# A sparse-attention and mixing kernel: a new issue order for all engines, two accumulator banks for the angles, sine products allowed on GpSimd

## The chip, the cores and the metric

The kernel runs on one core of a Trainium2 chip. The core has a matrix engine (TensorE, "PE" in the profile, with its weight loads "PEld"), three elementwise engines (VectorE "DVE", ScalarE "ACT", GpSimd "POOL") and a synchronisation engine (SyncE "SP") that issues all of this kernel's DMA transfers. Each engine takes its instructions in program order from a queue of its own and waits on semaphores for the results of the others. TensorE writes into PSUM, a small memory of eight banks; all else works in SBUF.

The metric is the device time of one execution in microseconds (us). A run is one execution that is timed.

## What is computed

Two stages follow one another. The first is attention with 4 batches, 8 heads, 768 positions and 64 channels a head. Each position sees its 31 nearest positions and 24 summaries of blocks of 32 positions (the maximum of the keys, the mean of the values). The second stage turns the 512 channels of each position by angles, mixes all positions, and ends with a channel product.

```python
scores_l = scale * np.matmul(q, k.transpose(0, 1, 3, 2))          # masked to |i - j| < 16
scores_s = scale * np.einsum('bhsd,bhnd->bhsn', q, k_sum) + np.log(block)
a = softmax(np.concatenate([scores_l_m, scores_s], axis=-1))
x = np.matmul(a, np.concatenate([v, v_sum], axis=2))              # then [B, S, 512]
theta = x @ w_theta
zr, zi = x * np.cos(theta), x * np.sin(theta)
y = np.einsum('ts,bsd->btd', w_tok_r, zr) + np.einsum('ts,bsd->btd', w_tok_i, zi)
u = x + y
out = u + np.maximum(u @ w_ch, 0.0)
```

## The kernel before

**Tiles.** Each batch has six tiles of 128 positions, 24 tiles in all, numbered b * 6 + i. A tile passes through these steps, each of them one or several operations:

- scores (line 1658): TensorE multiplies queries with 118 keys a query group: 94 neighbours and 24 summaries. VectorE adds the mask and takes the row's extreme (line 1684), ScalarE takes the exponentials (line 1688).
- the probabilities' transposition. For tiles 0 to 5 TensorE transposes them into the PSUM bank "p" (line 1693) and a copy brings them to SBUF (line 1516). From tile 6 on `turn_words` (line 1665) does it without TensorE: a copy splits each 32-bit word into 16-bit halves ("part", line 1516), one transposing DMA turns all of them (line 1674), and a second copy joins the halves ("join", line 1516, tiles `pt` and `zx`). There are 54 such transfers: two a tile for the probabilities, one a tile for x.
- the value product (line 1700), a small addition, a reciprocal and a multiplication that normalises (lines 1704 to 1713). The result is the tile's x.
- x is transposed in the same two ways (line 1725 or `turn_words`), split into a high part and a low part (lines 1516 and 1522), and stored to a scratch tensor in DRAM.
- angles (`theta_tile`, line 1751): twelve matmuls into the PSUM bank "t" (line 1757), a reduction to a full turn (lines 1765 to 1768), cosine and sine on ScalarE (lines 1779 and 1780), the products with x (line 1787, "sine products", two a tile, 48 in all), and their high and low parts (`split_z`).

High and low parts exist because TensorE's fast 32-bit product keeps fewer bits than the result needs. So a product of two 32-bit factors is made as three matmuls: high by high, high by low, low by high.

**Mixing.** `mix_step` (line 1803) adds one tile's share to three PSUM accumulators `m0` to `m2`. One batch needs two halves of six steps. Batch 0 uses line 1800, the other batches line 1835. At the end of a half, VectorE adds x back (line 1848) and the sum goes to DRAM. `out_unit` (line 1862) loads it again, splits it and makes the channel product (line 1878) with the last addition (line 1883); there are eight such units.

**Weights.** The weights come as 64-bit floats. `load_f64` (line 1551) decodes each of 32 pieces by hand: a magnitude (lines 1563 and 1565), two clamping and shifting steps (lines 1567 and 1568), two combining steps (lines 1570 and 1572), and the high and low parts.

**Order.** `Program.op` records each operation with its readers and writers and with the letters of the engines it may run on; it does not issue it. There are 2,460 operations. `Program.issue` (line 1477) then issues them in the order of the long string `ORDER` (from line 52 on). A row of it is an engine's letter (P, A, V, G, S for PE, ACT, DVE, POOL, SP) and a list of steps: "+2" means the operation two numbers after the last one. So the string fixes two things: the engine of each operation that may run on several, and the place of every operation in its engine's queue. 40 warm-up matmuls (line 1547) on a blank tile are part of the list.

The constant `DT = 6` in line 1491 is the tile from which the transposing transfers are used. `bank(tag, shape)` names a PSUM bank; a new user of a bank waits until the readers of the one before it are done.

```python
            for word in seqs:
                n = n + int(word[1:]) if word[0] == "+" else n - int(word[1:]) if word[0] == "-" else int(word)
                o = self.ops[n]
                o.fn(e)
```

Of the kernel before, what the change touches and what calls it, by code (L numbers as in the profile page):

```python
# [20 lines left out]
P = 128  # L21
# [32 lines left out]
V+1,+1,+1,+1,+1  # L54
A+1
G+1
V-107
S+43,+65
A+1
S-64  # L60
G-43
V+44,-2
S+3,-51
P+7,+1,+1,+1
S+43,+15
P-57,+1,+1,+1,+1
V+37,-47,+49
S+74,-127
V+113,+1
S-60,+2  # L70
P+18
V-4,+45
A+13
V-51
S-19,+4
V+29
S-31,-59
A+80
V-5,+40,-27,-16,+5
A+4,+13  # L80
S-31
G+65
V+1
S+21
A-34
V+14
A-38
V-18,+57,-42
A+43,-53
P-65  # L90
A+64
V+13,+26
A-22
V+38
S+213
P-292,+2,+2,+2,+2,+2
A+1,+6,+22
P-78,+67
V+69
S-81,-3,+51,+232,+398  # L100
V-596,+1
P+200
V-270,+71,+201,-200
A+196
G-283
P+16
V+1,+1,+268,+3
A+2,-203
P-60,-80,+1
G+140,+192  # L110
P-331,+1,+1
A+67
V+10,+259,+12
A-10,+3
V-242,+630,-380
A-9
P-262
A+274
P-351,+1
A+77  # L120
V+1,+252,+19
P-9,-339
S+111
A+1
S+31,+236
V-32
A+4,-1
P-349,+1,+1
S+212,+166
V-403,+100  # L130
A+274,-12
P-37,+79
G-285
S+227,-77
V-149,+1,+14
G+212
V-225
A+204,+1,-204
G+1
V+12,+192,+79  # L140
P-44,+12
V+44,+3,-58
S-183
P+149,+1
V+77
A-242
P+166,+1
V+72,+1
A+4,+2
V+9,-56  # L150
A+46,-2
V-242
A+209
P+37
V-47
A+59
P-399,+351
A-43
V-197,+31
A+255  # L160
V-3
A+4
V-255
G+166
A+91
S-285,+312,-240
P+243
V-318,+198
S+66
V-263,+275  # L170
A-77,+41
P-351
V+352,+1
P+35
A-77
V+121
P-78
V-211
S+107
A+105,+34  # L180
P-388,+1
G+111
P+287
V-256
A+212
V+75
S+283
G-357
V-212,+285
S-284,+281  # L190
V-115,+121
A-246
S+241,-266
V+228
A+47,-123
V+401,-271,+1
A-290,+293
P-89
V-171,+125
G-157  # L200
V+33,+257,-256
A+246,-2
V+13,-56,-234
A+244,+34
V-244
P+169,+1,+1
A+1
P+39
V-244
A+291  # L210
P-11
V-74,-205
A+292,-1,-47
V-87,+88
A+35
V-247
G+1
V+172
S+113
P+3  # L220
S-215
A-106
V+323
P-31
A-47
P-402,+403,+34
V+42,+2
S-4,+50
A-164
V+132  # L230
A-383
V+381,+1,-336,-45
A+291,-260,+220,+135,-49,+35,+12
P-496,+1,+1
A+495
V-2,-382,+368,-44,-323
G+627
V-337,+1
P+124
V-91  # L240
A+45,+2
V-370,+29,+221
P+42,+1,+1,+1
V-46,+75,-126
A+98
P+39,-447,+1
A+478
P+4
A+13,-48
S+249,+20,-530  # L250
V-45,+166,-195,+30,-29
A+42
G+1
V+252,+40
S+23
A-22
V+77,-383
A+1
V+265,+120
A-46,-73  # L260
P+40
A+1,+82,-81
P-451
V+156,+370,-382,+42
S+507,-572,+280
P+82,-482
G+186
P-185
V+155
G+295  # L270
P+2
V+242,-169
A-117,+315,-194,-168
V-205,+30,+1,+295,-294,+222,-1
A-252
P+336,-492,+1,+1,+450,+1
A+40
V-11
A+45,+193
V-182  # L280
P-84
V+29
P+11
S-204
V+401
P-119
V-77,+42,-1
A-81,-97
V+138
A-308  # L290
V+1
A+530
G-562,+204,+360
S-475,+454
G+23
A-197,+14,+1
G-85
P+115,-568,+1
V+453
A-338  # L300
P+411
G-410
A+377,+34,-73
P+40,+76
V+127
A-202
V-378,+418
S-20,-353,+532,-178
A+22,+1
V-421,+1  # L310
S+653
V-652,+1
P+599,-154
V+155
A-225
G+1
A-42
S-253
V+493,+28
S-31  # L320
P-164
A+1
G+216
A-20
P-185
V+182
P-223,+1,+1,+68
V-406,+577,+68,-84
S-278
V+11  # L330
S+252
V-16
G+88,-617
V+1
G+617
V-326
A+272
V-562,+1,+188
A+186,+186
P-225  # L340
A+224
V-196
S+170,-358
V+397,-208,-363,+569,+1
A-235,-95
G+96,+275
P-208,+3
G+206
P-238,+241
G-614  # L350
V+374,+1,-39,+40,+156
P-124
A-171,+324
P-184
V+1,+1,-88,+343,-3
S-98
A+40,-1
S-51
A+53,+1,+2
S-34  # L360
V-9,-500,+488,+20,-250
A-3
S+289
A-241,+1
G-98
P+171
V+198,+8,-582,+1,-10,+11,+302
P+64
G-165
P+168,-2,+3  # L370
G+138,-165
A+258
P-224,+123
A+1,+6
G-254,+381
P-261
V+208
A-277,+281
P-240,+1
V-345,+503,+67,-268  # L380
S+99,+123
A+1,-524
P+378
S+187,+62
A-31,-14
S-604
P+367,+1
S-296
V+253,-315,+316,-303
A+346  # L390
V-358,+1
P+535
V+1,-535
S-45
A+594,-593
V+580,+1
S-186,-340,+8
A+621
P-257,+3
A-385  # L400
V+585,-1
P-195,-1
V+214
A-14,+18
V-250,+245,-244
G-401,+682,-637
A+604,+36
P-263,+3
A+228,-582
V-70,+1,+616,-615  # L410
S+107
A+523
S+21
A-252
V-330,+1
P+520,-165
S+192
P+66,-255
V-427,+1
P+430  # L420
V+253
P-250
A+156,-191
V-329
G+562
A-581,+582,+18
V-60,+1,-192,-329,+629
G-648
V+649
G-86,+122  # L430
V-335,-330,+331,-350,+1,+19,+629
S-364,+107
A+148
S-151,+292
P-304,+3
S+201
P+18
A+1,-200
V+232
S-91  # L440
G+144,-385
V+301
S-540
V+585,-245,-53
P+35,+1,+3
V+215,-209
G+189
V+48
S+110
A-105,+51  # L450
S-63
V+10
A-659,+662,+51
G-712
V+1,+26
A+349
P+35
V+24,-58
A+190,+1
V-540,-26,+567,-566,+420  # L460
P-19,+3
A+255,-3,+5
P-56,+105
V+4,-108
P-199
V+5
G-386,+634
A-659,+671
V-670
A+672,+44  # L470
V-111,-579,+1
P+539,+1,+1,-145,+3,+143
A+37,+65,-629
V+668,-682,+403,+280,-2,-290
A+254,+42,-287
# [1507 lines left out]
```

## Time and profile before

| | us |
|---|---|
| runs: median (lowest to highest of 3) | 479.53 (478.3 to 482.27) |
| the profiled execution: its time | 477.79 |
| the profiled execution: its span | 475.9 |

The span runs from the first instruction to the last. The costliest groups of the profile, beside those that the prediction shows:

| line | engine | what | count | busy us |
|---|---|---|---|---|
| 1835 | PE | mixing, batches 1 to 3 | 864 | 162.1 |
| 1878 | PE | channel product | 256 and 128 | 65.7 and 43.4 |
| 1757 | PE | angles | 192 and 96 | 61.8 and 38.4 |
| 1800 | PE | mixing, batch 0 | 288 | 56.8 |
| 1688 | ACT | exponentials | 192 | 65.6 |
| 1684 | DVE | mask and row extreme | 192 | 46.4 |

In a group row of the profile, the line and the engine come first, then what is written and read (`zb<-xn,w`), the shape, the count, the busy time, the mean duration in ns, and the idle time of the engine just before. A row of one line or one tile gives the least, the median and the greatest duration in ns and the first and last start in us. Matmuls are pipelined, so their records overlap and the busy times of TensorE's groups are more than the time they take up. An engine that is idle without being the slowest costs nothing by itself.

### The profile page before, as it was taken

The page shows a single profiled execution, that of the slowest core. Times are in us where ns is not written, and L with a number is a line of the kernel's source. Part 1 is how long each engine was busy: PE and PEld are TensorE (multiplying, and loading weights), DVE is VectorE, ACT ScalarE, POOL GpSimd, SP SyncE. Part 2 cuts the span into 40 slices and gives each one's busy share as a digit, 9 for nine tenths or more (in the row PEclk, how much of TensorE's full clock was granted, in tenths as well). Part 3 has the DMA queues.
Part 4 walks back from the last instruction along what each step waited for, and adds up shares of the span by engine and source line. Part 5 has one row for each costly group of instructions (what it writes and reads, how often), then busy time and mean ns, then how long its engine had stood idle before and what let it go on. Part 6 is the DMA issues. An engine that isn't in the chain of part 4 may idle for free. (4 is left out here: it accounts for less than half of the span.)

```text
span 475.9 us, 10196 instructions
## 1 busy us (share of the span) xinstructions
PE 436.3 (92%) x3688; PEld 362.7 (76%) x3688; DVE 331.9 (70%) x1011; ACT 297.7 (63%) x587; POOL 169.8 (36%) x210
## 2 busy tenths in 40 slices
PE   1987868998899879999999999999999999999996
PEld 1565646776787668678887888878878889999996
DVE  4879999899997986675757758474555787333543
ACT  2579999999797979576876768579765221110110
POOL 1133126613333534656545464533220034231011
PEclk9999999999999999999999999999999999999999
DMA  8996476588589658968988597937835450635673
GB/s 301 332 340 188 149 256 207 137 263 212 121 231 216 140 155 163 240 181 188 205 264 193 117 228 141 206 85 182 157 86 130 160 190 31 203 118 191 213 224 128
DMA packets 108578, 88.89 MB, mean 187 GB/s; under 512 B 61936, under 2 KB 88304, under 8 KB 108528
## 3 DMA queue, kind: packets, MB, share of 16 engines
q1 hardware_dynamic: 108528, 88.24, 69.0%
q8 instruction: 29, 0.48, 0.4%
q14 instruction: 21, 0.17, 0.1%
HBM read 55.19 MB, written 18.87 MB: 156 GB/s over the span
## 5 line engine op out<-in xcount | busy, mean ns | idle before, releaser
L1835 PE MATMUL m<-wt,zq 128*128 128x512 f32 x864 | 162.1, 341 | 1.3 <-DVE ux L1848 1.3
L1835 PEld LDWEIGHTS m<-wt,zq 128*128 128x128 f32 x864 | 133.8, 189 | 22.3 <-DVE ux L1848 2.0
L1688 ACT ACTIVATE e<-e,st 128x118 f32<-128x118 f32 x192 | 65.6, 388 | 17.0 <-DVE st L1684 13.6
L1878 PE MATMUL c<-cuh,wth 128*128 128x384 f32 x256 | 65.7, 337 | 0.0
L1757 PE MATMUL t<-wth,xh 128*128 128x512 f32 x192 | 61.8, 403 | 2.3 <-ACT xh L1516 1.2
L1800 PE MATMUL m<-wt,zq 128*128 128x512 f32 (+1 forms) x288 | 56.8, 345 | 2.3 <-DVE ux L1848 1.2
L1516 ACT CAST cuh<-cu 128x384 fp32r<-128x384 f32 x21 | 10.0, 512 | 71.1 <-DMA cu<-u_scratch 57.0
L1684 DVE CUSTOM_DVE_ANT_0 e<-s,cs 128x118 f32<-128x118 f32 x192 | 46.4, 273 | 10.9 <-PE s L1658 4.4
L1800 PEld LDWEIGHTS m<-wt,zq 128*128 128x128 f32 x288 | 44.0, 189 | 10.3 <-DVE ux L1848 1.6
L1878 PEld LDWEIGHTS c<-cuh,wth 128*128 128x128 f32 x256 | 45.8, 188 | 0.9 <-POOL wth L1522 0.3
L1700 PEld LDWEIGHTS av<-v,pt 118*64 118x64 f32 x768 | 26.8, 137 | 24.8 <-issue 9.6
L1878 PE MATMUL c<-cul,wth 128*128 128x384 f32 x128 | 43.4, 339 | 0.0
L1700 PE MATMUL av<-v,pt 118*64 118x65 f32 x768 | 33.2, 227 | 10.5 <-ACT pt L1516 3.1
L1757 PEld LDWEIGHTS t<-wth,xh 128*128 128x128 f32 x192 | 33.9, 188 | 10.5 <-ACT xh L1516 1.8
L1757 PE MATMUL t<-wth,xl 128*128 128x512 f32 x96 | 38.4, 400 | 2.2 <-POOL xl L1522 1.5
L1883 DVE SCALAR_TENSOR_TENSOR cu<-c,cu 128x384 f32<-128x384 f32 x32 | 17.2, 554 | 30.2 <-PE c L1878 18.6
L1567 POOL TENSOR_SCALAR f<-f 128x512 f32<-128x512 f32 (+1 forms) x16 | 10.7, 671 | 74.9 <-DVE f L1565 38.1
L1516 POOL COPY pt<-zx 118x1024 uint16<-118x1024 uint16 x18 | 25.9, 1439 | 26.9 <-DMA zx<-zx 17.8
L1522 POOL TENSOR_TENSOR cul<-cu,cuh 128x384 fp32r<-128x384 f32 x16 | 16.6, 1049 | 50.8 <-ACT cuh L1516 24.4
L1522 POOL TENSOR_TENSOR zq<-zb,zq 128x512 fp32r<-128x512 f32 (+1 forms) x19 | 24.5, 1291 | 15.6 <-issue 6.6
L1765 ACT ACTIVATE w<-t,bmagic 128x512 f32<-128x512 f32 x24 | 16.4, 683 | 18.1 <-PE t L1757 9.2
L1787 DVE TENSOR_TENSOR w<-xn,w 128x512 f32<-128x512 f32 x18 | 13.9, 774 | 18.9 <-ACT w L1780 18.9
(104 smaller groups left out, 795.2 us busy)
## 6 DMA issues: line engine op xcount, KB each, us to landing
v<-vg SPq DMA_DIRECT2D x48, 195.0 KB, 3.7
q<-qg SPq DMA_DIRECT2D x24, 256.0 KB, 3.8
u_scratch<-zx SPq DMA_DIRECT2D x24, 256.0 KB, 3.2
cu<-u_scratch SPq DMA_DIRECT2D x32, 192.0 KB, 3.3
out<-cu SPq DMA_DIRECT2D x32, 192.0 KB, 2.2
kn<-kT SPq DMA_DIRECT2D x6, 798.0 KB, 6.4
ux<-u_scratch SPq DMA_DIRECT2D x16, 256.0 KB, 3.5
u_scratch<-ux SPq DMA_DIRECT2D x16, 256.0 KB, 3.4
```

Of the source, the lines that this page charges most:

```text
L1516: (nc.scalar.copy if e == "ACT" else V[e].tensor_copy)(dst, src)
L1522: op(f"VG tt {n}", lambda e: V[e].tensor_tensor(dst(), src(), hi().bitcast(F32), op=ALU.subtract), reads, writes)
L1684: op("V ttr", lambda eng, n=n: nc.vector.tensor_tensor_reduce(e.get()[:, n], sc[n % 2].get()[:, 2 * a + n // 2], mask(m), -SCALE, 3.0e38, ...
L1688: op("A exp", lambda eng, n=n: nc.scalar.activation(e.get()[:, n], e.get()[:, n], AF.Exp, bias=st.get()[:, n:n + 1], scale=-1.0), [(st, n) ...
L1700: mm("av", [lambda n=n, g=g: nc.tensor.matmul(xa.get()[ROW[g], n], t.get()[:, n, ROW[g]], v[g].get()[:NK, NH * a + n], start=True, stop=Tr ...
L1757: calls = [lambda t=t, xx=xx, k=k, c=c: nc.tensor.matmul(th.get(), xx.get()[:, c], w_th[c].get()[:, k], start=(c == 0 and t == 0), stop=(c ...
L1765: op(f"A psumb {DM}", lambda e: nc.scalar.activation(r(), th.get(), AF.Identity, bias=bmagic.get(), scale=1.0 / TWO_PI), [th, bmagic], [R])
L1787: op(f"V tt {DM}", lambda e, z=z, hc=hc: nc.vector.tensor_tensor(z(), xn[b, i].get().rearrange("p h d -> p (h d)")[:, None, hc].broadcast_ ...
L1800: nc.tensor.matmul(acc, zk(k, r, c), w_t[s, r, th].get()[:, kw], start=(clear and s == r == t == 0), stop=(s == NT - 1 and r == 1 and t == ...
L1835: nc.tensor.matmul((ma[c].get(), half(2, c)())[th], zk(k, r, c), w_t[s, r, th].get()[:, kw], start=(s == r == t == 0 and (th == 0 or c == 0)),
L1878: calls = [lambda t=t, k=k, uu=uu, c=c, co=co, acc=acc: nc.tensor.matmul(acc.get(), w_ch[c].get()[:, k, co * P:(co + 1) * P], uu.get()[:, ...
L1883: op(f"V ttp {HT}", lambda e, co=co, acc=acc: nc.vector.scalar_tensor_tensor(u.get()[:, co], acc.get(), 0.0, u.get()[:, co], ALU.max, ALU. ...
```

## The change

Three things change.

- The string `ORDER` is replaced as a whole. It lists the same 2,460 operations, and each may stand at another place and, where its letters allow it, on another engine. The transposing transfers and the 16-bit copies stay as many as they were.
- The angles of tile 6 and later use the PSUM bank "p" where the tile's number within its batch is odd, and the bank "t" where it is even. Before, all used "t".
- The sine products of line 1787 may run on GpSimd as well as on VectorE. In the new list 13 of the 48 do.

```diff
@@ -51,1369 +51,1387 @@
 ORDER = """
 S+104
-V+1,+1,+1,+1,+1
-A+1
-G+1
-V-107
-S+43,+65
...
+V+1,-101
+G+102
+V+1,+1,+1
+S-60,+79
...
@@ -1752,7 +1770,7 @@
 
         pr.key = ("TH", b * NT + i)
         x_h, x_l = xs_[b, i]
-        th = bank("t", [P, DM])
+        th = bank("p" if b * NT + i >= K["DT"] and i % 2 else "t", [P, DM])
...
@@ -1784,7 +1802,7 @@
-            op(f"V tt {DM}", lambda e, z=z, hc=hc: nc.vector.tensor_tensor(
+            op(f"VG tt {DM}", lambda e, z=z, hc=hc: V[e].tensor_tensor(
                 z(), xn[b, i].get().rearrange("p h d -> p (h d)")[:, None, hc].broadcast_to((P, 2, HC)), w.get()[:, :, hc], op=ALU.mult),
                [xn[b, i], w], [zb[b, h, i]])
```

In the new list the operations that may run on several engines are shared out as follows (old to new).

| operation | ACT | DVE | POOL |
|---|---|---|---|
| join of 16-bit halves (54) | 23 to 16 | 5 to 26 | 26 to 12 |
| split into 16-bit halves (54) | 30 to 25 | 6 to 11 | 18 to 18 |
| sine products (48) | | 48 to 35 | 0 to 13 |
| normalisation (48) | 9 to 8 | 39 to 40 | |
| all operations | 502 to 492 | 819 to 829 | 206 to 206 |

More of the change, by code (lines that the diff above doesn't have):

```diff
@@ L162 @@
[L162 to L367, printed above, removed]
@@ new lines @@
+G+1
+P-39
+V+4,-1,+13
+S-26,-63,+346
+V-256,+23
+P-57,+2
+V+17
+S+195
+V-196
+G+78
+P-92
+A+33,-13,-1
+V+74
+A-72
+V+7
+P-26,+2
+V+90,-63,+23,-111
+S+64
+V+88,+1
+A-62,-16
+S+272,-280
+V+45,+234
+A-284
+P+17
+V+1
+A+9
+G-24
+A+3,+24,+253
+P+5
+G-2
+V+6,-2,+1
+A-240
+G+41
+V+197
+P-270
+V+1
+S+262,-229
+A+242,+1
+V-275,+1,+265
+S+50
+P-306,-83,+1
+S+120,+48,+272
+V-85
+G-252
+V+251
+A-271
+V+274
+P-273
+V+272
+A-12,-239,+240,+13
+V-273,+1,+1
+P-86
+A+358
+G-253
+P+242
+A+13
+P-49
+A+1,+36,+11
+S-208
@@ new lines @@
+V+345,-135
+G+136
+V-345
+A+564,-272
+P+13
+A-45
+G+1
+V+1,+44,+202
+G+55
+P-176
+G+180
+V-260,+1
+S-313,+260
+P+133,+2
+S-28
+V-53,+205,-8,+17,-1,+2
+S-194,+16,+151
+G-134,+136
+A-236,+1
+P+125,-25
+A+146
+V-245,+260
+G-259
+A+246,-147
+V+144
+A+4
+G+17
+V-164
+P+25,+1
+A+136,-161
+P+27,-1
+V-46
+S-37
+V+197
+A+22,-262
+V+217
+A+27,+4
+V-204
+P+37
+S-350,+3
+A+348
+V-37,+168
+P+88,-173
+V-45,+1
+G-38
+V-45
+A+259
+P-36
+V+95
+A+4,+34,-132
+V+93
+S-69
+G-148
+S+1,+125
+P-179,+1,+1,+1
+V+270
+A-62
@@ new lines @@
+G+5
+S+1
+A+60
+P-195
+A+228,-108
+G+106
+V-54,-7
+S-248,+97
+V+160,+1
+A+3
+V+12
+A-28,+32
+P-195
+V+99
+G+3
+V-2
+P+22
+A-199,+270,-16
+G-253
+V+50,+149,+1,+50
+G-10
+A+16
+S+44
+A-249,+203
+S-201,+188
+A+65
+S-634
+V+329
+A+257
+G-1
+S-160,+162
+V-257,+50
+A-49
+P+75
+A+196
+P-195,+1
+G+133
+V-209,+269,-267,-1,+196,-194
+P+47,+27,-26,+1,+1,+157
+A-156
+V+157,+1
+P+91
+V+4,-252
+A+158
+P-134,-1
+V+245,-267
+G+200
+P-175
+V+239
+A-263,+1
+S+32,+144
+V+87
+P-64
+V+49
+A+4
+V-251,+2
+P+19
+V-18
@@ new lines @@
+V+1,+1
+S+39
+P+48
+G-140
+P+2,-214
+A+166,+151,-2
+G+4
+A-53
+V+88,+16,+2
+P-157,+1
+V+89
+P-88
+V+136,+3
+S-349,+313
+V-318
+A+372,-14,+16
+V-209
+A+51
+V+151,-8
+A+12,-16
+G-90
+S+1
+G+109,-158
+P+87,-307
+V+356
+A+4
+V-52
+A+51
+V-138,+88
+P-305,+2,-1
+G+265
+V+102
+A+4
+V+3,-16,-92
+S+2,+107
+V-108
+P-265
+V+2
+P+265,+1,+1,+1
+V-265
+A+210,+1
+G+1
+A+2
+V-211
+G+210
+V-207
+S+346,-16,-332
+V+294
+P+95,+1
+A-84
+P+1,+84,+1
+S-389
+G+208
+S+120
+A-69
+V+1
+A+45
+V-44,+45
+A+1
+G+1
+V-46,+100
@@ new lines @@
+V+1
+S+1
+P+15,+1
+V+1
+S-11
+P-117,+142
+S-13
+P+31,-6,-150,+1
+V+132
+S+35,-3
+V-31
+S+37
+V-34
+G-6
+P+20,+6,+1,-19,+20
+V+1
+A+9
+V-165,+166
+A-4
+S-151,+147
+P-18,+8,-7,+1,+1
+V+1
+P-8
+V+23
+P-22
+V+1
+P-137
+S+156,-18
+P+10
+V+1
+G+10
+S-9
+P+37
+V-20,+1
+P+1
+S-25,+49
+A+1
+S+2
+P-194
+G+193
+P-20
+V-13
+P+26,-12,+5,+1,-12,+1
+S+31
+P-30,+17
+V-16,-168
+P+172,+1
+S-4
+V+5
+P+4,+7
+V+1
+P-7
+A+13
+G+1
+V-13
+P-188
+S+202
+P+18
+S-37,+12,-6,-180
+P+217,-12,+13
+S+8
+A-29
+P+15
+V-18,+4,-3
@@ L1417 @@
+V+1
+S+1,-6
+P+25,+6,+6
+A-17,-3
+V+1
+P+25,+1
+A-21
+G+1
+P+8
+V-11
+P+12,+1
+V+1
+P+3
+S-2
+P+9,-19,+1,+19
+V+1
+S+1
+P-20
+V+1
+S+1
+P+9,+1
 V+1
```

2163 lines of the change are left out of this document (1039 added, 1124 removed).

## The prediction

> **What bounds the kernel now.** I read the page's totals first, then a table of stretches, then the waits of TensorE and the chain that ended last, and only then single groups.
>
> ```profile
> span 475.9 us, 10196 instructions
> PE 436.3 (92%) x3688; PEld 362.7 (76%) x3688; DVE 331.9 (70%) x1011; ACT 297.7 (63%) x587; POOL 169.8 (36%) x210
> ```
>
> TensorE is busy for 436.3 of 475.9 us, so 39.6 us of idle time are all that a new order can attack: no matmul is added or removed. The table of stretches says where they lie (columns: length, then busy time and instructions of each engine, granted clock, DMA share, GB/s):
>
> ```profile
> core 0: us, PE busy (x) PEld busy (x) DVE busy (x) ACT busy (x) POOL busy (x), PEclk, DMA share, GB/s
> 0.00:20.00 20.00, 10.33 (x84) 5.42 (x85) 12.23 (x38) 5.96 (x12) 2.55 (x7) 1.00 0.93 326
> 20.00:140.00 120.00, 103.86 (x1143) 79.71 (x1142) 112.30 (x373) 109.80 (x228) 40.26 (x57) 1.00 0.71 210
> 140.00:200.00 60.00, 53.41 (x464) 43.36 (x463) 46.40 (x151) 49.49 (x100) 28.67 (x32) 1.00 0.82 184
> 200.00:360.00 160.00, 157.13 (x1377) 129.83 (x1376) 101.55 (x342) 114.48 (x216) 74.70 (x92) 1.00 0.74 170
> 360.00:476.00 116.00, 111.61 (x627) 104.40 (x625) 59.44 (x111) 17.99 (x33) 23.61 (x23) 1.00 0.51 163
> ```
>
> TensorE idles 9.7 us in the first row, 16.1 in the second, 6.6 in the third, 2.9 in the fourth, 4.4 in the last. In the second row VectorE is busy for 112.3 of 120 us and ScalarE for 109.8 while TensorE has spare time: here the elementwise engines set the pace, VectorE first. In the third row no engine is full: what TensorE loses there are waits for single results. From 200 us on TensorE sets the pace. The waits and the end of the chain bear that out:
>
> ```profile
> PE m L1547 <- POOL zq L1545: 9.7, 1, 9.7
> PE av L1700 <- ACT pt L1516: 3.1, 6, 0.9
> PE t L1725 <- DVE w L1768: 2.2, 2, 1.6
> PE m L1800 <- DVE wt L1522: 0.9, 1, 0.9
> ...
> ```
> ```profile
> 367.84 10.61 PE m L1835 x60
> ...
> 446.89 25.35 PE c L1878 x144
> ...
> 472.33 0.56 DVE cu L1883
> ```
>
> The 9.7 us at the head are the memset ahead of the warm-up matmuls. After it the waits are small and many (the total in us, how often, the longest), the largest being attention's value product waiting for a copy out of the transposing path. The chain ends in unbroken matmuls; the last 3.7 us (after 472.2) are the last addition and store.
>
> **The change part by part.** All counts of the new order are taken from the two written lists of issue order, by adding up their entries: one entry is one operation of lines 1516 to 1885 on one engine.
>
> *1. VectorE's load ahead of the turning point.* I compare the lists at the same amount of TensorE work: the third mixing step of batch 0's second half, 100 us of matmul time into either list. In the trace it stands here:
>
> ```profile
> 136.21 2.99 PE L1800 MATMUL m<-wt,zq 128*128 128x512 f32 x18
> ```
>
> Ahead of that point the old list gives VectorE 326 operations, the new one 321. The kinds that differ, with the medians they cost:
>
> ```profile
> L1787 DVE TENSOR_TENSOR zb<-xn,w x30: 645/685/1777, 42.8 to 374.6; 128x512 f32<-128x512 f32 x30
> L1522 DVE TENSOR_TENSOR xl<-zx,xh x15: 679/693/1237, 30.4 to 364.4; 128x512 fp32r<-128x512 f32 x15
> L1568 DVE TENSOR_SCALAR f<-f x32: 274/421/1501, 5.3 to 395.0; 128x512 int32<-128x512 int32 x20, 128x256 int32<-128x256 int32 x12
> L1570 DVE SCALAR_TENSOR_TENSOR f<-wt,f x24: 376/620/1107, 22.6 to 157.2; 128x512 int32<-128x512 int32 x12, 128x256 int32<-128x256 int32 x12
> L1713 DVE TENSOR_TENSOR xn<-av,st x39: 409/424/425, 27.7 to 355.1; 128x256 f32<-128x256 f32 x39
> L1705 DVE TENSOR_SCALAR st<-av x24: 118/156/164, 24.2 to 354.7; 128x4 f32<-128x4 f32 x24
> L1516 DVE COPY pt<-p x3: 683/683/692, 22.0 to 39.4; 118x512 f32<-118x512 f32 x3
> L1516 DVE COPY v<-q x7: 369/408/593, 96.6 to 279.7; 24x512 f32<-24x512 f32 x7
> ```
> ```profile
> L1516 POOL COPY pt<-zx x18: 1348/1360/1842, 113.5 to 332.2; 118x1024 uint16<-118x1024 uint16 x18
> L1516 ACT COPY pt<-zx x16: 1340/1352/1376, 97.0 to 354.8; 118x1024 uint16<-118x1024 uint16 x16
> L1516 DVE COPY pt<-zx x2: 750/757/764, 268.2 to 344.6; 118x1024 uint16<-118x1024 uint16 x2
> L1516 DVE COPY zx<-zx x3: 724/755/1596, 224.5 to 328.9; 128x1024 uint16<-128x1024 uint16 x3
> L1516 DVE COPY zx<-xn x1: 685/685/685, 275.1 to 275.1; 128x1024 uint16<-128x1024 uint16 x1
> ```
>
> Gone from VectorE: four sine products (4 x 0.685 = 2.7), four 512-wide and three 256-wide steps of the weights' decoding (4 x 0.42 + 3 x 0.28 = 2.5), four 256-wide two-input steps of the same (4 x 0.4 = 1.6, just over the least of line 1570's row, which is its 256-wide form), one copy out of PSUM (0.7), two of v (0.8), one further step and two narrow casts (0.4 + 0.6). Together 9.3. Come to it: four normalisations (4 x 0.424 = 1.7), six small additions (0.9), two low parts of x (1.4), two join copies and one split copy of 16-bit halves (2 x 0.755 + 0.685 = 2.2), a cast and a reciprocal (0.4 + 0.2). Together 6.8. Net -2.5 us. VectorE has only 7.7 us of slack in the 120 us, so I take it whole: **-2.5**. Bounds: -7.7, which is all of that slack, and 0.
>
> *2. The 16-bit copies and the transposing transfers.* Of the 54 joins the old list gives 23 to ScalarE, 26 to GpSimd, 5 to VectorE; the new one 16, 12 and 26. A join takes 0.755 us on VectorE against 1.352 and 1.360, so the path from transfer to value product gets 0.6 us shorter 21 times. Nearly all lie behind the turning point. The wait that they belong to:
>
> ```profile
> L1674 SPq DMA_TRANSPOSE zx<-zx x54: 1231/1232/4018, 90.6 to 359.4; - x54
> ...
> DMA to landing us min/median/max: 3.0/3.5/9.8
> ```
> ```profile
> POOL pt L1516 <- DMA zx<-zx: 17.8, 8, 4.6
> ```
>
> The transfers stay 54, on SP, 1.23 us of issue each, 3.5 us to landing. GpSimd waited 17.8 us for them at the head of its queue, in eight waits, with other work behind. An order that knows those 3.5 us should not park an engine there. What that is worth to TensorE is not shown by any row; the bounds are the 6.6 us that it idles between 140 and 200 us, and 0. I take half, **-3.3**, as the copies are the largest single releaser among TensorE's waits but far from the only one. VectorE pays 21 x 0.755 = 15.9 us more, less what left it; its total rises by about 12 us. The cover is its idle time, 13.6 us between 140 and 200 us and 58.5 between 200 and 360: **0**. The cover is thinnest before 200 us, which is why I do not take more than half.
>
> *3. Sine products on GpSimd.* 13 of the 48 move, four of them ahead of the turning point. No row shows such a product on GpSimd; the nearest is its subtraction of the same shape:
>
> ```profile
> L1522 DVE TENSOR_TENSOR zq<-zb,zq x23: 412/685/1783, 58.7 to 394.4; 128x512 fp32r<-128x512 f32 x20, 128x256 fp32r<-128x256 f32 x3
> L1522 POOL TENSOR_TENSOR zq<-zb,zq x19: 732/1291/1733, 72.6 to 414.9; 128x512 fp32r<-128x512 f32 x16, 128x256 fp32r<-128x256 f32 x3
> ```
>
> So 1.29 us (at most 1.73) in place of 0.685: 0.6 us later for whoever needs it, the cast and low part behind it. GpSimd is busy for 40.3 of 120 us in that stretch; other work leaves it (two joins, two low parts of x, four small key copies), so its load grows by some 6 us only. Direct cost **0**, covered by the distance of most mixing steps behind their factors; where that is thin is the third rival.
>
> *4. Two banks for the angles.* From tile 6 on, odd tiles use the bank that the probabilities' transposes left. TensorE's rows for the angles wait for x's parts; the only wait for line 1768 is that of the early x transposes (2.2 us), which use the bank as before. **0**; it only loosens the order.
>
> *5. Head and tail.* In the new list 0.26 MB more (one value tile and a swapped weight) stand before q on SP's queue: at 326 GB/s 0.8 us later for the first scores, while VectorE has weights to decode. GpSimd's memset stood behind a low part of the first weight and now stands behind a decoding step of the second. The last addition and store are the same pair. **0**, bounds 0 and +0.8.
>
> Sum: -2.5 - 3.3 = -5.8 us. The profiled execution took 477.79 us for its span of 475.9; it becomes 472.0, span 470.1. The median of the runs shown, 479.53, lies 1.74 above the profiled one, so the forecast is **473.7**.
>
> **The rivals.**
> *The order fits throughout.* Half of VectorE's 7.7 us of slack before 140 us goes too (3.9), and all of the 6.6 after: -2.5 - 3.9 - 6.6 = -13.0, 466.5 us. For it: both losses are waits, not work. Against: VectorE at 94% leaves little to fill.
>
> *No change: the shared port eats it.* Blocked instructions show in the maxima: 1.777 for a sine product with median 0.685, 1.596 for a 16-bit copy with 0.755, each about 1 us over. If each of the four early products on GpSimd and each of the two early joins and the split costs VectorE some 0.5 us more, 3.5 us are added to its -2.5, and the 26 joins spoil the second stretch: 479.5 us. How often blocking strikes so far:
>
> ```profile
> L1522 DVE TENSOR_TENSOR zq<-zb,zq 128x512 fp32r<-128x512 f32 (+1 forms) x14 | 10.0, 716 | 0.1
> L1787 DVE TENSOR_TENSOR zb<-xn,w 128x512 f32<-128x512 f32 x13 | 8.9, 701 | 0.5 <-ACT w L1780 0.4
> ```
>
> Between 20 and 140 us the products' mean is 0.701 against a median of 0.685, so it strikes rarely; that keeps this rival below the forecast. The Trainium skill, "SBUF — State Buffer", section "Who interferes with whom", states it as a lock: a VectorE instruction with two SBUF inputs, or a copy in a two-port mode, and a GpSimd instruction that reads SBUF exclude each other for the whole of the one that came first. The maxima agree; the means say that the order so far seldom lets them meet. By that rule alone each moved product could cost VectorE its full 1.29 us, and the sum would be an estimated -2.5 + 4 x 1.29 = +2.7 before 140 us.
>
> *Slower: mixing waits for its factors.* In the new list batch 0's first mixing starts after 31.6 us of TensorE work instead of 44.4, and 14 of its 48 full-width steps stand under 2 us of TensorE work behind the last low part they need, where 4 did. If the ten extra each wait for one 1.29 us subtraction, that is +12.9, in TensorE's queue ahead of everything behind: -5.8 + 12.9 = +7.1, 486.6 us. From five of the ten on it outweighs the gain. Against: TensorE has 16 us of idle time in that stretch anyway, and such waits are 0.9 us in the trace.
>
> **How the numbers follow.** A measurement of this kernel tells about 1% (4.8 us) from no change. Forecast 0.42, with its own range 470.2 (-2.5 - 6.6) to 480.3 (0 + 0.8); fits throughout 0.16; port 0.26; mixing waits 0.16. The range runs from the second case, with 1.5 us to spare below it, up to 482, where the third begins to take hold: 465 to 482, leaving out about 0.2. Faster by over 1% (below 474.7): three quarters of the forecast, 0.32, and the second case, 0.16, with 0.02 of the port: 0.50. Slower by over 1%: 0.15 of the mixing case and 0.03 of the port: 0.18. Within 1%: 0.32.
>
> **What would show it.** Step 1: the same mixing step stands at 134 to 135 us instead of 137 and VectorE is still over 93% busy before it. Step 2: GpSimd's wait for the transposing transfers is well below 17.8 us and TensorE idles about 3 us between 140 and 200. Step 3: the products on GpSimd take 1.29 us, and VectorE's sine products keep a mean near 0.70. Step 4: no wait of the angles for line 1768. Wrong if VectorE's mean durations rise by over 0.05 us, if TensorE's waits for low parts (line 1522) exceed 5 us, or if the 140 to 200 us stretch still loses 6 us.

## The result and the profile after

The changed kernel took 457.96 us in the median (457.77 to 458.37, 4 runs), the kernel before 479.01 us beside it (478.3 to 482.27, 4 runs). The ratio is 0.9549, 95% interval 0.9504 to 0.9594: 4.5% faster. The forecast was 473.7 us and its range ended at 465. The sign was right; the gain was 21 us where 5.8 were forecast.

The profiled execution after took 457.85 us for a span of 456.0, which is 19.9 us less than before. The page's totals and the table of stretches, with the bounds that the prediction used as far as the shorter span allows:

```profile
span 456.0 us, 10212 instructions
PE 432.5 (95%) x3688; PEld 360.6 (79%) x3688; DVE 336.7 (74%) x1021; ACT 288.5 (63%) x574; POOL 167.3 (37%) x210
```
```profile
20.00:140.00 120.00, 112.04 (x1222) 87.05 (x1221) 114.65 (x397) 112.04 (x225) 48.59 (x65) 1.00 0.81 230
140.00:200.00 60.00, 57.63 (x559) 47.41 (x558) 54.24 (x169) 50.16 (x97) 31.24 (x42) 1.00 0.77 182
200.00:360.00 160.00, 159.26 (x1302) 132.69 (x1303) 106.57 (x331) 109.38 (x221) 64.02 (x73) 1.00 0.74 177
```

TensorE's idle time fell from 39.6 to 23.5 us, and its busy time, for the same 3,688 matmuls, from 436.3 to 432.5. So 16.1 us of the gain are idle time and 3.8 are not. Why the busy time fell is not shown: the granted clock is 1.00 in all these rows.

These stretches hold different work in the two kernels. For a fair comparison I took, for every step of TensorE, the matmul time that stands ahead of it in the list (each kind of step at its undisturbed time, 414 us in all) and the time at which it starts in the trace. The difference is how far TensorE has fallen behind its own work, called *lag* below:

```
matmul time ahead, us     0    20    60   100   160   200   300   410
lag before              9.7  15.4  31.7  38.0  49.6  51.2  55.9  57.2
lag after               9.1  13.9  24.7  28.3  33.0  34.3  36.8  37.6
gain                    0.6   1.5   7.0   9.7  16.6  16.9  19.1  19.6
```

The gain has three parts: 9.7 us up to 100 us of matmul time, 6.9 us between 100 and 160, and 3.0 after that. The points 20, 60, 100 and 160 stand at 35.4, 91.7, 138.0 and 209.6 us before and at 33.9, 84.7, 128.3 and 193.0 after. Here are the stretches between them, equal work in each pair, first before and then after (columns as in the prediction):

```profile
35.40:91.70 56.30, 46.39 (x556) 34.11 (x555) 53.59 (x170) 54.74 (x118) 21.45 (x28) 1.00 0.59 184
91.70:138.00 46.30, 42.22 (x358) 33.70 (x357) 44.26 (x143) 42.24 (x79) 14.47 (x24) 1.00 0.76 202
138.00:209.60 71.60, 64.39 (x574) 52.30 (x573) 55.21 (x181) 57.14 (x114) 34.47 (x38) 1.00 0.82 192
```
```profile
33.90:84.70 50.80, 44.91 (x496) 33.14 (x492) 49.94 (x157) 49.14 (x103) 20.19 (x25) 1.00 0.75 240
84.70:128.30 43.60, 42.01 (x371) 33.35 (x364) 41.91 (x150) 41.56 (x75) 20.18 (x31) 1.00 0.78 195
128.30:193.00 64.70, 62.52 (x566) 51.66 (x564) 59.02 (x189) 52.85 (x99) 32.19 (x43) 1.00 0.86 207
```

In the first two rows of each fence VectorE is busy for almost the whole stretch, and the stretch shortens as VectorE's busy time does: 53.59 to 49.94 and 44.26 to 41.91. ScalarE is as full in the first of them (54.74 of 56.30 us before, 49.14 of 50.80 after) and falls by as much: from 20 to 100 us of matmul time its busy time shrinks by 6.3 us, VectorE's by 6.0. So these rows name both engines and do not tell which of the two set the pace. In the third VectorE works more than before (59.02 against 55.21) and the stretch is 6.9 us shorter all the same: TensorE's idle time in it went from 7.2 to 2.2 us.

The waits after, TensorE's first (total, how often, longest), then the engines that wait for transposing transfers:

```profile
PE m L1565 <- POOL zq L1563: 9.1, 1, 9.1
PE av L1718 <- DVE xn L1731: 2.1, 3, 1.4
PE t L1743 <- DVE w L1786: 1.7, 2, 0.9
PE t L1775 <- ACT xh L1534: 1.5, 1, 1.5
...
PE t L1775 <- POOL xl L1540: 0.7, 1, 0.7
```
```profile
DVE zx L1534 <- DMA zx<-zx: 5.8, 4, 3.1
POOL pt L1534 <- DMA zx<-zx: 4.6, 3, 3.7
```

GpSimd's wait at a join of the probabilities fell from 17.8 us in eight waits to 4.6 in three. From the end of a split to the issue of its transfer the median is 0.06 us, where it was 1.1; the transfers themselves are as long as before.

### The profile page after: what moved, and what is told of

Read it like the earlier page. It is cut to its first block, busy times and chain, and to the rows that moved or that the text cites. A ratio compares the mean times of both kernels' runs of the same rounds, so it can differ in the third digit from the quotient of the medians.

```text
span 456.0 us, 10212 instructions
## 1 busy us (share of the span) xinstructions
PE 432.5 (95%) x3688; PEld 360.6 (79%) x3688; DVE 336.7 (74%) x1021; ACT 288.5 (63%) x574; POOL 167.3 (37%) x210
## 4 chain that ended last, share of the span: by engine, by line
PE 61%; DVE 18%; ACT 11%; issue 6%; DMA 3%; POOL 2%; DVEq 0%; POOLq 0%; ACTq 0%
PE m L1853 30%; PE c L1896 15%; PE p L1775 4%; PE t L1775 4%; PE av L1718 3%; PE s L1676 2%; DVE e L1702 2%; ACT e L1706 2%; DMA f<-vT 2%; DVE zq L1540 1%; PE av L1616 1%; DVE f L1590 1%; DVE f L1588 1%; ACT L1797 1%; DVE w L1786 1%
## 5 line engine op out<-in xcount | busy, mean ns | idle before, releaser
L1706 ACT ACTIVATE e<-e,st 128x118 f32<-128x118 f32 x192 | 65.9, 387 | 11.4 <-DVE st L1702 10.8
L1534 ACT CAST cuh<-cu 128x384 fp32r<-128x384 f32 x17 | 8.4, 512 | 60.4 <-DMA cu<-u_scratch 51.8
L1775 PE MATMUL t<-wth,xh 128*128 128x512 f32 x120 | 38.7, 404 | 1.5 <-ACT xh L1534 1.5
L1540 POOL TENSOR_TENSOR cul<-cu,cuh 128x384 fp32r<-128x384 f32 x15 | 15.5, 1047 | 66.4 <-ACT cuh L1534 37.4
L1540 POOL TENSOR_TENSOR zq<-zb,zq 128x512 fp32r<-128x512 f32 (+1 forms) x15 | 19.1, 1277 | 25.7 <-ACT zq L1534 14.8
L1585 POOL TENSOR_SCALAR f<-f 128x512 f32<-128x512 f32 (+1 forms) x23 | 13.5, 589 | 36.9 <-ACT f L1581 16.8
L1775 PEld LDWEIGHTS t<-wth,xh 128*128 128x128 f32 x120 | 21.4, 188 | 6.8 <-ACT xh L1534 1.9
L1775 PE MATMUL t<-wth,xl 128*128 128x512 f32 x60 | 24.1, 402 | 1.1 <-POOL xl L1540 0.7
L1896 PEld LDWEIGHTS c<-cul,wth 128*128 128x128 f32 x128 | 24.1, 188 | 0.3 <-POOL cul L1540 0.3
L1534 POOL COPY k<-kn 128x188 f32<-128x188 f32 x37 | 18.7, 513 | 12.9 <-PE s L1676 10.7
L1805 POOL TENSOR_TENSOR zb<-xn,w 128x512 f32<-128x512 f32 x12 | 17.6, 1466 | 15.0 <-ACT w L1798 15.0
```

Of the source, the lines that this page charges most:

```text
L1534: (nc.scalar.copy if e == "ACT" else V[e].tensor_copy)(dst, src)
L1540: op(f"VG tt {n}", lambda e: V[e].tensor_tensor(dst(), src(), hi().bitcast(F32), op=ALU.subtract), reads, writes)
L1585: op(f"VG ts {n}", lambda e: V[e].tensor_scalar(f(), f(), MOST, LEAST, ALU.min, ALU.max), [], [f_ref])
L1706: op("A exp", lambda eng, n=n: nc.scalar.activation(e.get()[:, n], e.get()[:, n], AF.Exp, bias=st.get()[:, n:n + 1], scale=-1.0), [(st, n) ...
L1775: calls = [lambda t=t, xx=xx, k=k, c=c: nc.tensor.matmul(th.get(), xx.get()[:, c], w_th[c].get()[:, k], start=(c == 0 and t == 0), stop=(c ...
L1805: op(f"VG tt {DM}", lambda e, z=z, hc=hc: V[e].tensor_tensor(z(), xn[b, i].get().rearrange("p h d -> p (h d)")[:, None, hc].broadcast_to(( ...
```

## The experiments

Theories at the start: VectorE's load ahead of the turning point makes the gain (the prediction's first term); the 16-bit copies and their transfers make it (the second term); or places and engines gain only together, as each was fitted to the other. The port was the rival against moved products. Line numbers shift between kernels. The last column is the mean, over a kernel's executions, of the matmul time lost to a lower granted clock: the time times one minus the mean clock. The kernel before has 3.8 us there, over 47 executions.

| run | us median | ratio to before (95%) | lost to clock, us |
|---|---|---|---|
| e1: new places, old engines | 538.87 | 1.1207 (1.1122 to 1.1292) | 28.7 |
| e2: old places, new engines | 545.33 | 1.1354 (1.1274 to 1.1433) | 30.9 |
| e3: new list for 94 us, then old | 474.12 | 0.9888 (0.9792 to 0.9984) | 2.7 |
| e4: old list for 94 us, then new | 470.91 | 0.9793 (0.9713 to 0.9874) | 5.1 |
| e5: new, one bank for the angles | 458.21 | 0.9587 (0.9542 to 0.9632) | 0.6 |
| e6: new, products all on VectorE | 463.42 | 0.9690 (0.9645 to 0.9735) | 2.2 |
| e7: new, 16-bit copies on old engines | 488.10 | 1.0208 (1.0156 to 1.0261) | 11.8 |
| e8: old, transfers early | 504.12 | 1.0544 (1.0465 to 1.0623) | 16.1 |
| e9: new, 11 more operations on GpSimd | 469.11 | 0.9779 (0.9737 to 0.9821) | 7.6 |
| e10: new, transfers late | 472.55 | 0.9862 (0.9798 to 0.9925) | 6.0 |
| e11: old, 13 products on GpSimd | 487.05 | 1.0157 (1.0119 to 1.0194) | 6.2 |
| e12: old, joins on new engines | 490.53 | 1.0219 (1.0153 to 1.0285) | 10.1 |
| e13: new, 12 low parts set to zero | 456.17 | 0.9535 (0.9473 to 0.9597) | 1.9 |
| e14: new, 6 operations into GpSimd's gaps | 464.51 | 0.9669 (0.9596 to 0.9743) | 2.8 |
| e15: old, 19 transfers earlier | 480.58 | 1.0028 (0.9987 to 1.0069) | 4.6 |
| e16: e9, TensorE kept busy | 476.45 | 0.9960 (0.9931 to 0.9990) | 7.5 |
| e17: e7, TensorE kept busy | 494.59 | 1.0329 (1.0284 to 1.0374) | 10.6 |
| e18: e1, TensorE kept busy | 553.62 | 1.1562 (1.1499 to 1.1624) | 31.8 |

### Places and engines (e1, e2)

e1 leaves each operation at its new place and gives it the old list's engine (378 differ); e2 does the reverse, with one bank. A few rows of e1's list against the changed kernel's, and of e2's against that before:

```diff
-V+1,-101
-G+102
-V+1,+1,+1
+V+1,-101,+102,+1,+1,+1
```

> The new list's places, but every operation on the engine that the old list gave it (no sine product on GpSimd, 5 joins on VectorE). Theory 'places': the 20 us come from where things stand in the queues, so most of it stays: 466 us or less. Rival 'engines': they come from the moves between engines, so most of it goes: 472 us or more. Third, 'only together': a list made for other engines fits badly, 478 us or more, as slow as before.

```diff
-A+1
+V+1
...
-V+113,+1
+G+113
+V+1
```

> The old list's places with the new list's engines and one bank for the angles. 'Places': no more than a few us gained, 474 us or more. 'Engines': 466 us or less. 'Only together': 479 us or more, slower than before.

Both are slower than either whole list, by 60 and 67 us against before. Neither half carries the gain alone; "only together" is right in kind. The losses are far larger than any theory had them, and part of them is the clock, see the last group.

### The two stretches (e3, e4)

One list up to 94 us of matmul time, then the other's order for what is left. The seam of e3, against the changed kernel's list:

```diff
-P-295,+230
-S-613,+24
+S-678,+24
...
+V+1,+1,+1,+1
```

> The new list up to 94 us of matmul time, the rest in the old list's order and engines. If each stretch's loss belongs to its own list, the gain of the first stretch (about 9 us) stays and the old loss between 100 and 160 us of matmul time comes back: 469 to 471 us. If the later loss is a debt of the slow first stretch, it does not come back: 462 us or less.

> The old list up to 94 us of matmul time, then the new one. If each stretch's loss belongs to its own list: the 9 us of the first stretch are lost again, the later 10 us stay, 467 to 469 us. If the later loss is a debt of the slow first stretch, it comes back too: 475 us or more.

e3 has the new lag at 90 us (26.8, new 28.2) and between 100 and 160 loses 11.4, as the old list does (11.6); e4 has the old lag at 90 (35.0, old 36.0) and then loses 3.2, less even than the new list (4.7). So up to 160 us each stretch's loss belongs to the list in that stretch, not to what came before, and e4 wins nothing back of what it lost early. After 160 us this does not hold for e3: it loses 12.7 us there, the old list 7.6. Of the difference 1.7 us are matmul time lost to a drop of the clock at 252 us; the rest is not explained. Around the seam both lose some. So the two gains don't add up exactly, and both medians lie 2 to 3 us above the range that the fitting theory gave them.

### The small parts: banks and products (e5, e6, e11)

```diff
-        th = bank("p" if b * NT + i >= K["DT"] and i % 2 else "t", [P, DM])
+        th = bank("t", [P, DM])
```

> The new list, with all angles in the one bank that the kernel before used. In both lists the matmuls of a tile's angles stand behind the last reader of the tile before, so a second bank should free little. 'Bank is only room': 457.5 to 460 us. Rival 'the bank carries part of the gain': 462 us or more, with waits of line 1775 for the reading of the bank.

e5 is within 0.25 us of the changed kernel: the second bank is worth nothing.

e6 takes the 13 sine products back to VectorE in the new list; e11 moves the same 13 to GpSimd in the old one.

```diff
-V-289
-G+168
+V-289,+168
```

> The new list, with the 13 sine products of GpSimd given back to VectorE at the same places. 'Load': VectorE has four of them (4 x 0.69 us) more in the stretch in which it is nearly always busy, and the others only push its queue: 460 to 466 us. Rival 'port': VectorE is blocked less by GpSimd, which pays for it: 458 us or less. 'Only together': a list made for other engines fits badly, 470 us or more.

```diff
-V-171,+125
-G-157
+V-171
+G+125,-157
```

> The old list and engines, with only the 13 sine products moved to GpSimd that the new list has there. 'Load': VectorE has four products less in the first stretch and more room after it, 473 to 476 us. 'Only together': the old list gave GpSimd other work at those places, 480 us or more.

In the new list the move is worth 5.5 us. e6's stretch from 20 to 60 us of matmul time, to hold against the changed kernel's 50.80 with VectorE busy 49.94:

```profile
33.60:87.10 53.50, 46.77 (x494) 34.23 (x491) 52.38 (x159) 49.09 (x103) 16.59 (x22) 0.97 0.69 218
```

VectorE is 2.4 us busier and the stretch 2.7 us longer. Of the 2.7 us, 1.9 are busy time of TensorE, at a mean clock of 0.97, and 0.8 idle time, so this row alone does not show that VectorE's load made it longer. In the old list the same move costs 7.6 us. The groups of e11's products:

```profile
L1800 POOL TENSOR_TENSOR zb<-xn,w 128x512 f32<-128x512 f32 x12 | 19.4, 1620 | 27.7 <-ACT w L1793 27.7
L1800 DVE TENSOR_TENSOR zb<-xn,w 128x512 f32<-128x512 f32 x18 | 16.1, 899 | 0.1
```

and of the changed kernel's:

```profile
L1805 POOL TENSOR_TENSOR zb<-xn,w 128x512 f32<-128x512 f32 x12 | 17.6, 1466 | 15.0 <-ACT w L1798 15.0
L1805 DVE TENSOR_TENSOR zb<-xn,w 128x512 f32<-128x512 f32 x18 | 13.3, 746 | 1.1 <-ACT w L1798 1.1
```

The same instructions take 1,620 and 899 ns in the mean in the one list, 1,466 and 746 in the other. Over all of VectorE's operations ahead of the 100 us point, the time above each kind's median is 11.3 us in e11, 4.4 before and 2.3 after. In e11, beside each of the four products ahead of that point, one VectorE instruction takes 1.36 to 1.76 us where its kind takes 0.4 to 0.7. In the changed kernel the four take 1.30 us each and none beside them is slowed like that. So the port rival is real: in the old places it took back the 2.8 us of work that the move saved, and more. The new list puts the early products where they do not meet; behind that point four of the other nine still take 1.75 to 1.81 us.

### The 16-bit copies and the transfers (e7, e12, e8, e10, e15)

e7 is the new list with the copies on the old list's engines (64 of 108 differ); e12 the old list with the joins on the new list's engines (35 differ).

```diff
-V+161,-14,+58,-57
+A+161
+V-14,+58,-57
```

> The new list's places; the splits and joins of 16-bit halves go back to the engines that the old list gave them (64 of 108 change engine; 5 joins on VectorE where the new list has 26). If the short joins on VectorE are the core of the gain: 472 to 480 us. If they are worth little: 462 us or less. If any other share of engines spoils the places: 490 us or more.

```diff
-A+594,-593
+V+594
+A-593
```

> The old list and engines, with only the joins of 16-bit halves on the engines that the new list gives them (35 of 54 change, 26 on VectorE). If the short joins alone carry the gain after the first stretch: 470 to 474 us. 'Only together': 485 us or more.

e7 is 30 us slower than the changed kernel, 2 us short of the range for spoilt places; of the parts that were taken back alone none costs as much. Its waits show where (all engines):

```profile
POOL pt L1555 <- DMA zx<-zx: 17.5, 5, 11.2
POOL zx L1555 <- DMA zx<-zx: 15.0, 5, 4.8
```

GpSimd stands again at the head of its queue for transfers. But the same joins in the old places make that list 11 us slower. So cheaper joins alone are no gain.

The transfers themselves: e8 puts each on SP's queue right behind its split in the old list, e15 moves only 19 ahead, e10 moves 41 in the new list up to two places back, on SP alone. One row of each:

```diff
-S-34
+S+1,-35
```

> The old list with its engines; on SyncE's queue each transposing transfer stands right behind the split that feeds it, nothing else is moved. In the trace of the kernel before the transfer was issued 1.1 us (median) behind its split, in the changed one 0.06 us. 'Transfers stood too late': 470 to 475 us. Rival 'not the transfers': 477 to 480 us. If they hold up other transfers: 481 us or more.

```diff
-S-34
+S+1,-16,-19
```

> The old list and engines; 19 transposing transfers move ahead of transfers that SyncE issued, in the trace of the kernel before, after their split was already done. Late transfers in the new list cost 14.6 us for 1.5 us more of mean distance between split and transfer (e10). 'The transfers' place sets the stretch after 100 us': the mean distance falls by about 1 us, 470 to 474 us. Rival 'they are late because of something else': 477 us or more.

```diff
-S+278,-619,+536
+S+278,-619,+592
```

> The new list; on SyncE's queue 41 of the 54 transposing transfers stand up to two transfers later, nothing else is moved. 'The path through the transfers is what TensorE waits for': each is late by 0.5 to 2 us, and with it the join and the value product, 465 us or more. Rival 'the path has room': 457.5 to 460 us.

e8 blocks SP's queue. Its waits, and those of the kernel before:

```profile
SPq L1702 <- ACT zx L1544: 35.8, 10, 8.8
SPq L1702 <- ACT e L1716: 21.5, 6, 9.1
```
```profile
SPq L1674 <- ACT zx L1516: 22.0, 6, 5.3
```

A transfer that stands too early waits with all later loads behind it. In e10, too late, the mean from a split's end to its transfer's issue is 2.56 us, against 1.08 in the changed kernel. Its lag is the new list's up to 100 us (28.3, 28.3), where few transfers have been issued, and 12 us more at the end (49.5, 37.6):

```profile
128.30:196.70 68.40, 63.21 (x565) 51.50 (x564) 58.31 (x189) 52.97 (x100) 32.13 (x43) 1.00 0.81 193
```

That is the stretch that took 64.70. Of the 6.9 us that the new list gains between 100 and 160, 3.7 are lost again by the transfers' places alone. The other 8.2 us of e10's lag arise after 160 us, where the new list gained 3.0. In e15 split to transfer falls from 1.87 to 1.36 us in the mean, but transfer to join rises from 5.88 to 6.22: the joins stand where they stood, and the time is that of before. So the place of a transfer matters once the joins behind it are placed for it.

### VectorE's load (e9, e14, e13)

If VectorE's load alone set the first 100 us, moving more of it away must help. e9 moves 11 operations to GpSimd; e14 moves six and puts each into a gap of GpSimd's trace; e13 replaces 12 low parts of weights by a constant.

```diff
-V-287
+G-287
```

> The new list with eleven more VectorE operations of the first stretch moved to GpSimd at the same places: three sine products, one low part of z and seven low parts of weights, each with 8 us or more of matmul time before its first user. 'VectorE's load sets the first stretch': 11 x about 0.65 us less there, 451 to 454 us. If GpSimd's slower work (1.3 us each) or blocking eats it: 456 to 460 us. 'Only together': 462 us or more.

```diff
-V-289
-G+168
+G-121
```

> The new list; six VectorE operations (four low parts of weights, two sine products) go to GpSimd, each into a gap of its queue of 1.8 to 6.6 us that the changed kernel's trace shows, with the operands ready by then. 'VectorE's work sets the first stretch': five of them lie there, 5 x 0.69 us less: 453 to 456 us, faster than the changed kernel. 'Only the fit' or blocking: 458 us or more.

```diff
+            if at in ZERO:
+                V[e].memset(dst().bitcast(F32), 0.0)
```

> The new list; twelve low parts of weights in the first stretch are not computed but set to zero by VectorE, at their places (the low parts of pieces 2, 3, 4, 7, 8, 9, 11, 12, 13, 18, 19 and 20 are left out). 'VectorE's work sets the first stretch': each saves the difference between a 0.69 us subtraction (0.42 for the three narrow ones) and a fill of about 0.2 us, 5 us in all: 452 to 454 us. 'Only the fit of the queues': 457 us or more.

e9's stretch from 20 to 60 us of matmul time, and e14's:

```profile
34.60:93.50 58.90, 49.80 (x493) 37.02 (x489) 49.45 (x153) 49.58 (x104) 29.43 (x32) 0.88 0.64 204
```
```profile
35.20:89.10 53.90, 46.38 (x496) 33.96 (x494) 51.30 (x152) 49.35 (x103) 26.85 (x29) 0.97 0.70 219
```

In e9 VectorE has 9.5 us to spare and the stretch is 8.1 us longer: results come late from GpSimd (VectorE waits 5.7 us for it there, ScalarE 3.5) and TensorE waits. Of the 8.1 us, 3.2 are idle time of TensorE and 4.9 its busy time at a mean clock of 0.88. In e14 VectorE's operations ahead of the 100 us point sum up to 130.6 us by their medians, 5.5 less than in the changed kernel, but run 6.8 us above their medians where that had 2.3, and the rest goes into waits. Load is a bound, not a price list. e13 gives no other engine more to do. But its fill cost more than the 0.2 us that was expected:

```profile
L1544 DVE MEMSET wt<- x10: 272/485/485, 39.7 to 125.1; 128x512 f32 x7, 128x256 f32 x3
```

At 0.49 us (0.27 for the narrow ones) the twelve save 2.3 us by these medians and not 5. The stretch from 60 to 100 us is 41.0 us against 43.6, that from 20 to 60 us 50.6 against 50.8, at a mean clock of 0.97; ahead of it 4.5 us were lost in the profiled execution, with the clock down there. Over its runs e13 is 1.8 us below the changed kernel. That fits a saving of 2.3 us, but it lies within e13's own spread (454.82 to 459.71) and outside the ranges of both theories.

Of the two nearly full engines all three relieve VectorE alone. ScalarE is busy for 49.14 of the changed kernel's 50.80 us between 20 and 60 us, and no run takes work from it alone. As long as that work stays, the stretch has 1.7 us to give, whatever VectorE's load is. So ScalarE's load remains an untested rival for the first gain.

### The granted clock (e16, e17, e18)

Every experiment but e5 had stretches at half clock in its profiled execution; the two executions compared above had none before their last 3.1 us. One of e9's, with the gap ahead of it:

```profile
70.80:74.20 3.40, 0.00 (x0) 0.00 (x0) 1.58 (x2) 3.37 (x10) 3.40 (x4) 0.83 0.00 0
74.20:79.80 5.60, 5.56 (x29) 4.56 (x30) 5.19 (x13) 4.33 (x13) 3.29 (x5) 0.50 0.56 168
```

TensorE idles for 3.4 us, waiting for a normalisation, and then runs at 0.50. To tell the wait from the clock, three kernels were given small matmuls in TensorE's gaps:

```diff
+                for _ in range(FILL.get(n, 0)):
+                    self.filler()
                 o.fn(e)
```

> The changed order with the same eleven operations moved to GpSimd as in the earlier kernel, and 63 small matmuls of 40 columns added on TensorE where it idled 1.8, 2.3 and 3.4 us there (45, 56 and 71 us); they read constants and write columns that nothing reads, so the result is unchanged. In that kernel's profile the granted clock fell to 0.50 for 6.8 us behind each of the last two gaps: 6.8 us of matmul time lost. Clock theory: the gaps cost more than their length because the clock falls behind them; kept busy, TensorE keeps its clock there and the 469.1 us become 462 to 465. Order theory: VectorE's and GpSimd's places in the queues set the time whatever the clock does: the clock is 1.0 in that stretch, the time stays 467 to 470.

> The changed order with the 16-bit copies on the old list's engines, as before, and 72 such small matmuls in six gaps of TensorE (153, 178, 243, 288, 301 and 355 us). Its earlier profile shows the clock at 0.50 for 3.4 us behind the second, and 6.8 us each at the third and fifth: 8.5 us of matmul time lost. Clock theory: 488.1 becomes 480 to 483. Order theory: 486 to 490.

> The changed places with every operation on the old list's engine, as before, and 162 such small matmuls in nine of its 18 gaps (those where the scores' bank is free to write: 21, 48, 94, 184, 192, 209, 294, 335 and 353 us). Its earlier profile has ten drops, 54.6 us at half clock, 27.3 us of matmul time. Clock theory: five or six of the drops go, 538.9 becomes 520 to 528. Order theory: 535 to 540, since what is waited for is the elementwise engines' results.

These fail as a test. A filler took 0.23 us where I had reckoned with 0.1. The first two groups in e16's timeline (start, length, count of records, two a filler):

```profile
45.43 3.44 PE L1565 MATMUL s<-cs 128*128 128x40 f32 x30
...
58.17 4.43 PE L1565 MATMUL s<-cs 128*128 128x40 f32 x38
```

With the third group (6.8 us) they run for 14.7 us in 7.5 us of gaps, and the kernel is 7.3 us slower, which is about the surplus. The clock lost as much as without them (7.5 against 7.6). Part of that is the small matmuls' own doing. In the first of these two rows of e16 nothing else runs on TensorE, and the next row is at half clock:

```profile
77.70:81.10 3.40, 3.40 (x33) 3.40 (x32) 0.74 (x1) 1.66 (x5) 0.19 (x1) 1.00 0.91 256
81.10:84.50 3.40, 3.40 (x25) 2.81 (x25) 1.64 (x6) 0.00 (x0) 0.38 (x2) 0.50 0.02 6
```

So the split between wait and clock isn't settled by intervention. What there is is the spread between executions: over 84 executions of the 18 kernels, each kernel about its own mean, the time rises by 0.64 us (0.46 to 0.83) for each us of matmul time lost to the clock. By that and the last column of the table, the clock would account for some 16 of the 60 us that e1 loses against before, for 8 of 25 in e8, 4 of 11 in e12, and 7 of the 30 that e7 loses against the changed kernel. These are estimates: the slope comes from scatter of a few us within kernels.

## Why the prediction was wrong

**Step 1, VectorE's load: the term that failed most.** It was -2.5 us (bounds -7.7 and 0); the traces have -9.7 at that point. The place was right: from 33.9 to 128.3 us VectorE is busy for 91.9 of 94.4 us. The step that failed reads "Ahead of that point the old list gives VectorE 326 operations, the new one 321". That compares the lists at one point. The loss is made earlier: at 60 us of matmul time the entries differ by 7.8 us and the lag by 7.0. In e4 and e16 TensorE does not win back later what it lost, so a difference on the way can cost more than the last one shows; that the largest one sets the price is not tested.

ScalarE's load has no term, though the prediction read it as nearly as full (109.8 of 120 us). The sum charges VectorE with four normalisations and six small additions, but three of the former and all of the latter came from ScalarE, and ScalarE's busy time between 20 and 100 us fell by 6.3 us, VectorE's by 6.0. How the 9.7 us divide between the two engines is open.

And the sum held work alone. VectorE had started 317 operations at the 100 us point instead of 324, which is -4.3 us by medians; the time above the medians fell by 2.1; waits and the rest by 3.3. e14 shows that the last two are not minor: they ate a saving of 5.5 us of work. The point in that mixing step, foretold for 134 to 135 us, stands at 128.3.

**Step 2, copies and transfers: right in kind, too small.** It was -3.3 out of bounds of -6.6 and 0; the stretch gave 6.9. Half was taken "as the copies are the largest single releaser among TensorE's waits but far from the only one". With the copies on the old engines (e7) it takes about 6 us longer, 1.7 of them lost to the clock, and with the transfers late (e10) 3.7 us longer, so it hangs on both. The bound was wrong too: idle time in it fell by 5.0 us and TensorE's busy time by 1.9. As foretold, GpSimd's wait is well below 17.8 us and TensorE idles 2.4 us (3 foretold) between 140 and 200. The cover for VectorE's extra work held: 5.7 us of its idle time are left there, 16.4 before.

**Step 3, sine products on GpSimd.** The price was right, 1.306 us in the median (1.29). The direct cost of 0 held only because of where the new list puts them: e11 pays for the same products in other places.

**Steps 4 and 5, banks, head and tail.** Right: 0 for the banks (e5); the head moved by -0.6 us.

**From 200 us on** the prediction took nothing, as TensorE sets the pace there. 3.0 us came from there; no run took that part alone.

**"39.6 us of idle time are all that a new order can attack"** was wrong: 16.1 came from idle time, 3.8 from busy time.

**The rivals.** The nearest was "the order fits throughout" at -13.0; it lacked the third part and the falling busy time. The port is real (e11), but costs nothing in the new places ahead of the 100 us point. Mixing did not wait for its factors: TensorE's largest wait for a low part after is 0.7 us.

**The clock** plays a small part: the kernel before loses 3.8 us of matmul time to it on average, the changed one and e5 together 0.9 over eight executions. At 0.64 that is some 2 of the 21 us between the medians, and nothing between the two profiled executions.

**Still open:** which detail of the fit is worth how much. Taken back alone, the copies, the transfers' places and the products cost 30.1, 14.6 and 5.5 us, 50 us of a gain of 21, so the 9.7 and 6.9 us can't be divided further by such moves.

## What to carry to other kernels

When two written orders are compared by load, add it up for every engine that is nearly full, at many points of equal work on the slowest engine, and look at the largest difference as well as the last: what that engine had lost by 90 us was not won back in e4. In an order with fixed queues, an operation's place and its engine are one choice: move the one without the other and the queues block. Look at the granted clock of each experiment before a slower time is put down to what was moved.

## What the runs showed of the hardware

- The clock falls behind short gaps. In e7 TensorE was busy for 0.74 of the 2.4 us ahead of a drop; the 3.4 us before that were full:

```profile
174.60:178.00 3.40, 3.37 (x59) 2.65 (x57) 0.78 (x7) 3.37 (x7) 1.56 (x4) 1.00 0.83 179
178.00:179.10 1.10, 0.05 (x1) 0.05 (x1) 0.61 (x2) 1.10 (x5) 1.10 (x4) 1.00 1.16 394
179.10:180.40 1.30, 0.69 (x2) 0.25 (x2) 1.30 (x1) 0.18 (x1) 1.30 (x2) 1.00 0.77 214
180.40:183.80 3.40, 3.06 (x7) 2.48 (x8) 1.90 (x7) 2.22 (x3) 0.48 (x1) 0.50 0.43 114
```

  The Trainium skill, "TensorE: Matmul & The Clock Gate", section "Part 1: The HAM clock gate (the "warmup" mystery)", states a free-running window of about 3.4 us and half clock after an idle one. The traces agree on the factor of 0.50 and on stretches of 3.4 us and multiples of it. But a window need not be empty here to count as idle: the 3.4 us up to the drop hold 1.7 us of work.
- The drops lie on a fixed grid. In each of the 13 traces with two or more of them they start whole multiples of 3.413 us apart, to within 0.005 us. I divided the 17 traces that have a drop into windows of that length, counted from a drop both ways, without the first and last 12 us and without windows already at half clock. All 50 windows in which TensorE was busy for less than 1.5 us were followed by half clock, 14 of 49 between 1.5 and 2.1 us, and six of 2,089 above that. Those six are full of the small matmuls of e16 to e18. Windows that held such matmuls and about 0.8 us or more of other work kept the clock when they began at full clock.
- Whether a given gap costs the clock varies between executions of one kernel, as it may fall differently on that grid (not shown, as one execution of each kernel has a trace): the mean clock of the kernel before lay between 0.982 and 1.000.
- A sine product that meets VectorE on GpSimd is slowed as VectorE's is. The rows of that line in e11 and in the changed kernel (least, median, greatest in ns):

```profile
L1800 POOL TENSOR_TENSOR zb<-xn,w x12: 1295/1756/2005, 43.5 to 379.8; 128x512 f32<-128x512 f32 x12
```
```profile
L1805 POOL TENSOR_TENSOR zb<-xn,w x12: 1299/1306/1811, 40.7 to 351.9; 128x512 f32<-128x512 f32 x12
```

  The same product takes 0.45 us more in the median where the list lets the two engines meet. That agrees with the Trainium skill, "SBUF — State Buffer", section "Who interferes with whom", by which the two engines exclude each other, whichever came first.
